# A list scheduler given a more detailed timing model, and a table of priority offsets emptied

## The chip, the cores and the metric

The kernel runs on one core of a Trainium2 chip, as one launch. The metric is the time of one execution on the device in microseconds; the median of several executions counts. Times within the program come from one execution recorded by the hardware profiler. TensorE is called PE, VectorE DVE, ScalarE ACT, GpSimd POOL and SyncE SP, as in the profile.

## The reference

A recurrent attention feeds a two-layer MLP. There are 4 x 8 = 32 heads, 768 positions and 40 features per head:

```python
for t in range(S):
    y[:, :, t] = np.einsum('bhd,bhde->bhe', rt, state)
    Sa = np.einsum('bhde,bhe->bhd', state, at)
    state_decay = state * wt[:, :, None, :] - np.einsum('bhd,bhe->bhde', Sa, bt)
    state = state_decay + np.einsum('bhd,bhe->bhde', vt, kt)
...
x = np.ascontiguousarray(attn_out.transpose(0, 2, 1, 3)).reshape(B * S, H * D)
h = x @ w_in
sp = np.where(h > 20.0, h, np.log1p(np.exp(np.minimum(h, 20.0))))
g = h * np.tanh(sp)
return (g @ w_out).astype(np.float32)
```

`x` is 3072 x 320, `w_in` 320 x 2048, `w_out` 2048 x 320.

## The kernel before

The 768 positions are cut into 12 chunks of 64. Within a chunk the recurrence becomes matrix products and the inverse of a triangular matrix; only the state goes from chunk to chunk. The heads are split into two halves, `be`, and the sixteen pairs of heads of a step into two groups, `g`.

Four kinds of work make up the attention:

- **A fetch**, `pre_a(c, be)`, lines 126 to 203: two loads each of `wa` and `bk` on SP; two scans on DVE (L147, L157) that give the running products of the decays; products of those with a, b and k (L152, L170); eight matmuls of 128 x 128 by 128 x 168 (L186), whose result is taken apart by ACT and DVE (L188 to L193) into `GP` and `HA`; and eight transposes (L202). It writes the running products `P` to memory (L172, POOL's queue). Four fetches serve two chunks.
- **An inversion**, `pre_inv(n)` and `post_inv(n, ...)`, lines 205 to 260, for two chunks at once. First DVE alone: a transpose (L209), thirty rounds of a product and a sum, each needing the one before (L214, L216), and two more transposes (L218, L220). Then PE and ACT put the inverted blocks together (L232, L241, L249 to L251) and multiply them into `KT` (L258, L260).
- **A step**, `step(c)`, lines 265 to 370: the recurrence itself. Its parts run for both groups in the order of `SORD`: `a` brings the state and the values to PE (L277, L284, L286), `b` makes the masked products (L314, L316), `u` and `d` transpose (L293, L304), `c` makes the output and the new state (L334, L339, L342, L343, L346). At its end the loads of the next step are issued on POOL's queue, and the output of the chunk goes to memory (L370).
- **The conversion of the MLP's weights**, `split` and `load_f32`, lines 445 to 516: a piece is loaded to `cv_d` by SP, turned into float32 by one ACT and three DVE instructions (L459 to L463), and split into a high and a low part (L494, L495). `M.early()` does the first of four quarters of `w_in` (3 pieces), `M.first()` the other three (9 pieces), `M.second()` 3 pieces of `w_out`, `M.third()` the last 5. The buffers of `M.first()` lie where those of the fetches were, so it waits for the last fetch; its pieces share one `cv_d`.

The MLP, `Mlp.run`, goes over 12 blocks of 256 rows. `load_x` reads the attention's output back and splits it. For each quarter `q` of the hidden layer, 32 matmuls of 128 x 128 by 128 x 256 (L583) are followed by Mish on ACT (L585), a split (L588, L589), and, three quarters later, 24 matmuls by 320 columns (L603 to L605).

The program is written in one order: fetches 0 to 3, inversion 0, fetches for the next pair, `M.early()`, and then for each pair n of steps, by `ORDER = '0aiA1'`: step 2n, the four fetches of pair n + 2, inversion n + 1, (in the fifth pair) `M.first()`, step 2n + 1. `M.second()` stands ahead of the sixth pair, the MLP at the end.

That is not the order on the engines. At the end of `TileContext` a list scheduler runs the program against a timing model and picks, whenever an engine can take an instruction, the ready one with the best priority. It thereby fixes every engine's queue; on the chip each queue runs in that order, held by semaphores. The priority is the place in the program, and `at(tc, k)` (line 44) changes it for a block: a positive entry of the table `OFF` moves the block forward by about that many places, a negative one back. The keys name the blocks: `I` and `I0` to `I5` the start of an inversion, `J5` and `T1` its second part, `p4` and `P00` to `P11` the fetches, `s0` to `s10` steps, `b0`, `c0`, `u0`, `u1`, `d0`, `d1` parts of every step, `E`, `W` and `V` the three conversions. The model is the framework's default one, which prices each engine's instructions more simply than the other model that it offers.

Most tiles have two buffers, `XL` and `TT` of the inversion one; PSUM has two each for fetches, inversions and the two kinds of step product. Those limits hold whatever the priorities.

Of the kernel before, what the change touches and what calls it, by code (L numbers as in the profile page):

```python
# [34 lines left out]
LA = 2  # L35
ORDER = '0aiA1'

OFF = {'I': 80, 'T1': 80, 'P00': -40, 'P10': 80, 'P11': 40, 'b0': 15, 'c0': 600, 'u0': -15, 'u1': 250, 'd0': 250,
       'd1': 150, 'W': 600, 'V': 400, 'E': 150, 'I0': 600, 'I1': -15, 'I2': 15, 'I3': 150, 'I4': 80, 'p4': 15,
       'I5': -150, 'J5': 600, 's0': 150, 's2': -15, 's3': 80, 's4': 250, 's6': -15, 's7': -40, 's8': 150, 's10': -150}  # L40
SORD = 'a0 b0 u0 d0 a1 b1 u1 d1 c0 c1'


def at(tc, k):
    return tc.high_priority(offset=OFF[k]) if OFF.get(k) else nullcontext()


def layouts(inp, S=768):
    nch = S // C

    def v(x):
        return x[:, :, :S].reshape(4, 2, 2, 2, nch, C, 40)

    r, k, vv, w, a, b = (v(inp[n]) for n in 'rkvwab')
    o = {}
    wt = w.transpose(4, 2, 1, 6, 3, 0, 5).reshape(nch, 2, 2, 40, 8, C)
    wa = np.zeros(wt.shape[:4] + (1040,), np.float32)
    wa[..., :520].reshape(wt.shape[:4] + (8, 65))[..., 1:] = wt
    wa[..., 528:] = a.transpose(4, 2, 1, 6, 3, 0, 5).reshape(nch, 2, 2, 40, 512)
    o['wa'] = wa  # L60
    bt, kt = (x.transpose(4, 2, 1, 6, 3, 0, 5).reshape(nch, 2, 2, 40, 8, 1, C) for x in (b, k))
    bk = np.concatenate([bt, kt], -2)
    bk[:, 1] = np.concatenate([kt, bt], -2)[:, 1]
    o['bk'] = bk.reshape(nch, 2, 2, 40, 8, 128)
    o['rD'] = np.ascontiguousarray(r.transpose(4, 1, 6, 2, 3, 0, 5)).reshape(nch, 2, 40, 16, C)
    o['vD'] = np.ascontiguousarray(vv.transpose(4, 1, 6, 3, 0, 2, 5)).reshape(nch, 2, 40, 8, 128)
    o['vN'] = np.ascontiguousarray(vv.transpose(4, 2, 5, 3, 0, 1, 6)).reshape(nch, 2, C, 16, 40)
    p = np.arange(128)
    cst = np.zeros((128, 328), np.float32)
    cst[:, :128] = np.eye(128)  # L70
    cst[:, 128:192] = (p[:, None] % 64) < np.arange(64)
    cst[:, 192:256] = np.arange(64) < (p[:, None] // 64) * 32 + p[:, None] % 32
    cst[:, 256:296] = (p[:, None] % 64) == np.arange(40)
    cst[:, 296:328] = np.arange(32) < p[:, None] % 32
    o['cst'] = cst
    return o
# [356 lines left out]
def mlp_layouts(inp):  # L433
    wi, wo = inp['moe_w_in'], inp['moe_w_out']
    wi = wi.reshape(2, 2, 2, 40, 2048).transpose(1, 3, 0, 2, 4).reshape(320, 2048)
    a = np.empty((128, 3, 2048), wi.dtype)
    a[:, 0], a[:, 1] = wi[0:128], wi[128:256]
    a[0:64, 2] = a[64:128, 2] = wi[256:320]
    o = {'wi': a.reshape(128, 3, 4, 512).transpose(0, 2, 1, 3), 'wo': wo.reshape(16, 128, 320).transpose(1, 0, 2)}
    o = {n: np.ascontiguousarray(x).reshape(128, -1) for n, x in o.items()}  # L440

    return {n: x.view(np.int64) if x.dtype == np.float64 else x for n, x in o.items()}
# [185 lines left out]
def build(tc, I, out, nch):  # L628
    with ExitStack() as ctx:
        dp = ctx.enter_context(tc.tile_pool(name="dp", bufs=1, space=bass.MemoryType.DRAM))  # L630
        yD = dp.tile([nch, 2, 40, 2, 512], F32, name="yD")
        pD = dp.tile([nch, 2, 40, 2, 520], F32, name="pD")
        M = Mlp(ctx, tc, I, yD, pD, out)
        with ExitStack() as actx:
            attention(actx, tc, I, yD, pD, nch, M)
        M.run(nch)


def launch(**inputs):
    import concourse.bacc as bacc  # L640
    import concourse.tile as tile
    from concourse.bass_utils import run_bass_kernel_spmd

    nch = inputs['r'].shape[2] // C
    arrays = layouts(inputs, nch * C)
    arrays.update(mlp_layouts(inputs))
    nc = bacc.Bacc("TRN2", target_bir_lowering=False, num_devices=1)
    I = {n: nc.dram_tensor("in_" + n, x.shape, mybir.dt.from_np(x.dtype), kind="ExternalInput").ap() for n, x in arrays.items()}
    out = nc.dram_tensor("out_0", (nch * 256, 320), F32, kind="ExternalOutput").ap()
    with tile.TileContext(nc) as tc:  # L650
        build(tc, I, out, nch)
    res = run_bass_kernel_spmd(nc, [{"in_" + n: x for n, x in arrays.items()}], core_ids=[0]).results[0]["out_0"]
    return np.ascontiguousarray(res.reshape(nch, 4, C, 320).transpose(1, 0, 2, 3)).reshape(nch * 256, 320)
# [4 lines left out]
```

## Time and profile before

| What | Value |
|---|---|
| median of 3 runs | 839.51 us (836.24 to 843.57) |
| profiled execution: its span | 843.5 us; the highest of the 3 runs is 843.57 |
| instructions | 18796 |
| PE matmul busy | 748.6 us (89%) |
| PE weight load busy | 695.6 us (82%) |
| DVE busy | 462.0 us (55%) |
| ACT busy | 429.0 us (51%) |
| POOL busy | 103.3 us (12%) |
| DMA | 61.91 MB, mean 73 GB/s |

Shares over the whole span mix stages with different limits, so they are read by stage. In a row of a group of instructions, the columns are: line, engine, operation, output <- inputs, shape and count, then busy time in us with the mean of one in ns, then the idle time of the engine just before them and what ended it. In a row of the timeline: start, length, engine, line, operation, and how many were merged. In a row of stretches: the stretch, its length, the busy time of each engine (with its count of instructions), the granted clock of PE as a share of full speed, the share of the DMA engines, GB/s.

### The profile page before, as it was taken

The page shows a single profiled execution, that of the slowest core. Times are in us where ns is not written, and L with a number is a line of the kernel's source. Part 1 is how long each engine was busy: PE and PEld are TensorE (multiplying, and loading weights), DVE is VectorE, ACT ScalarE, POOL GpSimd, SP SyncE. Part 2 cuts the span into 40 slices and gives each one's busy share as a digit, 9 for nine tenths or more (in the row PEclk, how much of TensorE's full clock was granted, in tenths as well). Part 3 has the DMA queues.
Part 4 walks back from the last instruction along what each step waited for, and adds up shares of the span by engine and source line. Part 5 has one row for each costly group of instructions (what it writes and reads, how often), then busy time and mean ns, then how long its engine had stood idle before and what let it go on. Part 6 is the DMA issues. An engine that isn't in the chain of part 4 may idle for free.

```text
span 843.5 us, 18796 instructions
## 1 busy us (share of the span) xinstructions
PE 748.6 (89%) x7816; PEld 695.6 (82%) x7816; DVE 462.0 (55%) x975; ACT 429.0 (51%) x937; POOL 103.3 (12%) x182
## 2 busy tenths in 40 slices
PE   2645898998989889889799899999999999999998
PEld 2534697887868778778768799999999999999998
DVE  6789879739899658788924639221222222122110
ACT  4533647774586866566738546333333333333331
POOL 8100012113122023221101200000000000000000
PEclk9855689899999999899959999999999999999999
DMA  6422223323423233323425734211120111100000
GB/s 177 134 71 64 74 63 73 90 67 105 129 81 80 66 88 103 82 67 96 123 66 142 179 109 128 54 35 36 38 54 25 31 54 35 35 21 16 16 1 32
DMA packets 58212, 61.91 MB, mean 73 GB/s; under 512 B 25536, under 2 KB 48704, under 8 KB 58128
## 3 DMA queue, kind: packets, MB, share of 16 engines
q1 hardware_dynamic: 49296, 40.94, 17.6%
q0 software_dynamic: 8832, 19.79, 9.5%
q8 instruction: 61, 1.00, 0.5%
q14 instruction: 23, 0.19, 0.1%
HBM read 48.79 MB, written 11.86 MB: 72 GB/s over the span
## 4 chain that ended last, share of the span: by engine, by line
PE 62%; DVE 15%; ACT 15%; issue 5%; DMA 2%; ACTq 0%; DVEq 0%; SPq 0%
PE ph L583 21%; PE po L604 7%; PE po L605 7%; PE po L603 7%; PE pa L186 5%; PE pa L258 4%; PE pq L314 3%; PE pq L334 2%; DVE XL L216 2%; DVE tmp L214 2%; ACT ad L155 2%; PE pu L284 1%; DMA cv_d<-in_wo 1%; DVE P L147 1%; ACT bdT L250 1%
## 5 line engine op out<-in xcount | busy, mean ns | idle before, releaser
L583 PE MATMUL ph<-xh,w_ih 128*128 128x256 f32 x576 | 148.3, 283 | 0.5 <-ACT xh L566 0.5
L585 ACT ACTIVATE g<-ph 128x512 f32<-128x512 f32 x96 | 57.3, 598 | 179.3 <-PE ph L583 179.2
L589 DVE TENSOR_TENSOR gl<-g,gh 128x1024 fp32r<-128x1024 f32 x48 | 58.7, 1225 | 160.7 <-ACT gh L588 160.4
L583 PE MATMUL ph<-xh,w_il 128*128 128x256 f32 x576 | 123.6, 283 | 0.0
L186 PE MATMUL pa<-bk,ad 128*128 128x168 f32 x384 | 85.0, 373 | 42.7 <-DVE bk L170 15.0
L604 PE MATMUL po<-w_ol,gh 128*128 128x320 f32 x384 | 118.8, 310 | 0.1
L605 PE MATMUL po<-w_oh,gl 128*128 128x320 f32 x384 | 118.4, 309 | 0.0
L603 PE MATMUL po<-w_oh,gh 128*128 128x320 f32 x384 | 117.7, 309 | 0.0
L186 PEld LDWEIGHTS pa<-bk,ad 128*128 128x128 f32 x384 | 70.8, 233 | 47.8 <-issue 22.8
L583 PEld LDWEIGHTS ph<-xh,w_ih 128*128 128x128 f32 x576 | 109.3, 190 | 0.7 <-ACT xh L566 0.7
L583 PE MATMUL ph<-xl,w_ih 128*128 128x256 f32 x384 | 101.2, 285 | 0.0
L583 PEld LDWEIGHTS ph<-xh,w_il 128*128 128x128 f32 x576 | 96.3, 190 | 0.0
L583 PEld LDWEIGHTS ph<-xl,w_ih 128*128 128x128 f32 x384 | 73.1, 190 | 0.8 <-issue 0.5
L604 PEld LDWEIGHTS po<-w_ol,gh 128*128 128x128 f32 x384 | 72.1, 188 | 0.5 <-DVE w_ol L495 0.5
L605 PEld LDWEIGHTS po<-w_oh,gl 128*128 128x128 f32 x384 | 72.1, 188 | 0.1
L603 PEld LDWEIGHTS po<-w_oh,gh 128*128 128x128 f32 x384 | 71.8, 188 | 0.0
L258 PE MATMUL pa<-bdT,HA 128*104 128x128 f32 x384 | 57.0, 304 | 9.0 <-ACT bdT L251 7.3
L258 PEld LDWEIGHTS pa<-bdT,HA 128*104 128x104 f32 x384 | 49.9, 190 | 14.4 <-ACT bdT L251 9.1
L216 DVE TENSOR_TENSOR XL<-XL,tmp 128x30 f32<-128x30 f32 (+9 forms) x180 | 59.0, 328 | 2.4
L214 DVE TENSOR_TENSOR tmp<-XL 128x30 f32<-128x30 f32 (+9 forms) x180 | 58.5, 325 | 2.5
L314 PE MATMUL pq<-bdr,UVT 128*128 128x128 f32 x384 | 57.3, 294 | 2.3 <-DVE UVQ L316 1.5
L314 PEld LDWEIGHTS pq<-bdr,UVT 128*128 128x128 f32 x384 | 50.8, 205 | 4.0 <-DVE UVQ L316 1.9
(89 smaller groups left out, 1243.5 us busy)
## 6 DMA issues: line engine op xcount, KB each, us to landing
wa<-in_wa SPq DMA_DIRECT2D x48, 162.5 KB
bk<-in_bk SPq DMA_DIRECT2D x48, 160.0 KB
cv_d<-in_wi SPq DMA_DIRECT2D x12, 512.0 KB
cv_d<-in_wo SPq DMA_DIRECT2D x8, 640.0 KB
pD<-P POOLq DMA_DIRECT2D x48, 81.2 KB, 2.2
VS<-in_vN POOLq DMA_DIRECT2D x24, 160.0 KB, 3.6
UVT<-in_vD POOLq DMA_DIRECT2D x24, 160.0 KB, 3.9
bdr<-in_rD POOLq DMA_DIRECT2D x24, 160.0 KB, 4.4
```

The costliest lines, as they stand in the source:

```text
L155: A.copy(ad[q, :, :, al], a[q].rearrange("p (s k t) -> p s k t", k=2, t=32))
L186: PE.matmul(pt[:, j], ad[:, s0 + j].rearrange("p k a t -> p (k a t)"), bk[:, s0 + j], start=(j == 0), stop=True, skip_group_check=True)
L214: V.tensor_tensor(out=tv, in0=X[:, i + 1:32, i:i + 1].broadcast_to([128, 31 - i, i]), in1=X[:, i:i + 1, 0:i].broadcast_to([128, 31 - i, i] ...
L216: V.tensor_tensor(out=X[:, i + 1:32, 0:i], in0=X[:, i + 1:32, 0:i], in1=tv, op=ALU.add)
L258: PE.matmul(pk[:, j], ha[:, s0 + j], bd[:, s0 + j].rearrange("p a t -> p (a t)"), start=(j == 0), stop=True, skip_group_check=True)
L314: PE.matmul(pq[:, s], UVT[:, g * 4 + s, be * 128:be * 128 + 128], br[:, be, g * 4 + s].rearrange("p a t -> p (a t)"), start=(s == 0), stop ...
L583: PE.matmul(o, w, x, start=(j == 0 and n == 0), stop=(n == 7), skip_group_check=True)
L585: A.activation(g[:, f0:f0 + 2], ph, AF.Mish)
L589: V.tensor_tensor(out=gl, in0=g, in1=gh.bitcast(F32), op=ALU.subtract)
L603: PE.matmul(po[k], gh[:, j, t], oh, start=(f == 0), stop=False, skip_group_check=True)
L604: PE.matmul(po[k], gh[:, j, t], ol, start=False, stop=False, skip_group_check=True)
L605: PE.matmul(po[k], gl[:, j, t], oh, start=False, stop=(f == 15), skip_group_check=True)
```

## The change

The scheduler is told to run the program against the framework's more detailed timing model, and the table of offsets is emptied, so that every block has the priority of its place in the program. The function `at` stays and now does nothing. No instruction is added or removed; tiles, buffers, the order of the program and the assignment to engines and queues stay.

```diff
-OFF = {'I': 80, 'T1': 80, 'P00': -40, 'P10': 80, 'P11': 40, 'b0': 15, 'c0': 600, 'u0': -15, 'u1': 250, 'd0': 250,
-       'd1': 150, 'W': 600, 'V': 400, 'E': 150, 'I0': 600, 'I1': -15, 'I2': 15, 'I3': 150, 'I4': 80, 'p4': 15,
-       'I5': -150, 'J5': 600, 's0': 150, 's2': -15, 's3': 80, 's4': 250, 's6': -15, 's7': -40, 's8': 150, 's10': -150}
+OFF = {}
...
-    with tile.TileContext(nc) as tc:
+    with tile.TileContext(nc, schedule_with_timeline_sim=True) as tc:
         build(tc, I, out, nch)
```

## The prediction

> **What bounds the kernel now.** I read the times of the engines by stage first, then the waits inside the stage that has slack, then the timeline where a chain looked stretched. The stages, with busy time by engine and the granted clock of TensorE:
>
> ```profile
> core 0: us, PE busy (x) PEld busy (x) DVE busy (x) ACT busy (x) POOL busy (x), PEclk, DMA share, GB/s
> 0.00:42.00 42.00, 18.65 (x88) 15.82 (x88) 28.99 (x54) 22.14 (x54) 19.55 (x36) 0.91 0.56 156
> 42.00:105.00 63.00, 36.81 (x266) 30.98 (x267) 56.97 (x139) 27.21 (x79) 5.07 (x10) 0.61 0.23 69
> 105.00:421.00 316.00, 279.15 (x4005) 247.78 (x4004) 251.88 (x632) 212.06 (x541) 67.87 (x120) 0.96 0.34 88
> 421.00:484.00 63.00, 58.23 (x680) 46.61 (x682) 28.60 (x51) 36.70 (x75) 9.86 (x14) 0.84 0.50 125
> 484.00:843.50 359.50, 355.75 (x2786) 354.45 (x2780) 95.59 (x102) 130.93 (x191) 1.00 (x2) 1.00 0.15 43
> ```
>
> The last row is the MLP with the end of the attention: PE is busy for 355.75 of 359.50 us at a clock of 1.00. No order of the queues can shorten it; it only shifts. All that the change can move lies before 484 us. There VectorE sets the start (56.97 of 63 us), and between 105 and 421 us two engines share the limit: PE 279 of 316 us (88%), VectorE 252 (80%). Neither is full, so this stage is limited by the order of its work, and that is what is replaced. What VectorE waits for there and to 484 us:
>
> ```profile
> engine line waited for: us in total, times, longest us
> DVE stn L342 <- PE pq L339: 23.2, 9, 7.7
> DVE UVQ L316 <- PE pq L314: 21.0, 12, 4.6
> DVE HA L191 <- ACT HA L190: 13.9, 17, 2.5
> ```
>
> The two longest, 44.2 us together, are waits for the recurrent steps' own products, not for the work fetched ahead. The steps are thus what the stage can least afford to delay.
>
> **The change part by part.** Nothing is added to or removed from any engine; I take every instruction's duration as it stands, so the sum has only waits. The sum is made against the profiled execution, 843.5 us; the highest of the three runs shown is 843.57 and the median 839.51, so 4.0 us are taken off at the end.
>
> First, the start. The first inversion (30 rounds of L214 and L216) hangs on the first four fetches and stands before the next four in the program too, so it had first call on VectorE with its offset and still has it without. Here is how it ran (timeline of VectorE, first and last lines):
>
> ```profile
> 49.87 2.09 DVE L209 STREAM_TRANSPOSE XL<-GP 128x1024 f32<-128x1024 f32 x1
> 51.84 1.20 DVE L147 TENSOR_TENSOR_SCAN P<-wa,d 128x520 f32<-128x520 f32 x1
> 52.99 0.17 DVE L214 TENSOR_TENSOR tmp<-XL 128x30 f32<-128x30 f32 x1
> 53.02 0.09 DVE L210 MEMSET XL<- 128x32 f32 x1
> 53.08 0.17 DVE L150 COPY w<-P 128x8 f32<-128x8 f32 x1
> 53.15 0.69 DVE L152 TENSOR_TENSOR wa<-wa,P 128x512 f32<-128x512 f32 x1
> 53.75 0.20 DVE L216 TENSOR_TENSOR XL<-XL,tmp 128x30 f32<-128x30 f32 x1
> ...
> 97.25 1.93 DVE L218 STREAM_TRANSPOSE TT<-XL 128x1024 f32<-128x1024 f32 x1
> ```
>
> ```profile
> L216 DVE TENSOR_TENSOR XL<-XL,tmp 128x30 f32<-128x30 f32 (+9 forms) x180 | 59.0, 328 | 2.4
> L214 DVE TENSOR_TENSOR tmp<-XL 128x30 f32<-128x30 f32 (+9 forms) x180 | 58.5, 325 | 2.5
> ```
>
> Its own work is 2.09 + 0.09 + 30 x (0.328 + 0.325) = 21.8 us, but it took 97.25 - 49.87 = 47.4 us, because other ready work was queued after nearly each link. So 25.6 us of fetch work sits inside the chain. Offsets did not prevent that; only the model's view of when a link is ready could. Bounds: 0 if the new model sees it alike, -25.6 if it keeps the chain whole and all of that reaches the end. I take 0, because the inserted work has to be done on the same engine anyway and VectorE is the bound of that stage.
>
> Second, the offsets of the steps and of their parts (`s0`, `s4`, `c0` with 600 and the rest; s2, s6, s7 and s10, being negative, only put steps back). Without them a step with an odd number stands behind four fetches (some 200 instructions, counted in the code) and an inversion (some 260). Its chain has 10 VectorE instructions: 4 of L316, 4 of L342, 2 of L346. Each may now find one longer instruction ahead of it:
>
> ```profile
> L147 DVE TENSOR_TENSOR_SCAN P<-wa,d 128x520 f32<-128x520 f32 x24 | 29.6, 1233 | 0.3
> L170 DVE TENSOR_TENSOR bk<-bk,wa 128x1024 f32<-128x1024 f32 x24 | 29.1, 1214 | 0.1
> ```
>
> That is 10 x 1.23 = 12.3 us for a step at most and 61.5 us for the five (1, 3, 5, 7 and 9), if each lies on the path; 0 if each meets nothing new. What hides it is the PE work fetched ahead, which keeps PE at 88%. Since two thirds of what VectorE idles between 105 and 421 us (316.0 - 251.9 = 64.1) has the size of the step waits above, I count a third as exposed: +20.
>
> Third, `W`, `V` and `E`, which drew the conversion of the MLP's weights forward. SyncE and the chain of the end show it (start, length, what):
>
> ```profile
> 376.11 72.58 SPq L453 DMA_DIRECT2D cv_d<-in_wi  x9
> 455.05 0.33 SPq L453 DMA_DIRECT2D cv_d<-in_wo  x1
> ```
>
> ```profile
> 462.89 3.83 DMA cv_d<-in_wo
> 471.60 4.50 DMA cv_d<-in_wo
> 481.69 0.74 ACT w_oh L494
> ```
>
> Twelve pieces pass through one buffer from 376.1 to 482.4 us, 8.9 us each. Without the offset the first nine stand behind the last inversion on VectorE: at worst they start its own 21.8 us later; at best, once it is done, they run at their own pace. That pace comes from the transfer above and these rows (376 to 484 us):
>
> ```profile
> L463 DVE SCALAR_TENSOR_TENSOR cv_w<-cv_d,cv_w 128x512 int32<-128x512 int32 (+1 forms) x12 | 8.7, 721 | 0.1
> L462 DVE SCALAR_TENSOR_TENSOR cv_w<-cv_m,cv_w 128x512 int32<-128x512 int32 (+1 forms) x12 | 8.6, 719 | 0.2
> L459 ACT ACTIVATE cv_m<-cv_d 128x512 f32<-128x512 f32 (+1 forms) x12 | 8.5, 704 | 2.3 <-DMA cv_d<-in_wi 2.1
> L461 DVE TENSOR_SCALAR cv_w<-cv_m 128x512 int32<-128x512 int32 (+1 forms) x12 | 5.3, 441 | 10.5 <-ACT cv_m L459 10.4
> ```
>
> 3.83 + 0.70 + 0.44 + 0.72 + 0.72 = 6.4 us, so 12 x 2.5 = 30 us could be won back. Bounds -30 to +22; I take +5, near the middle, because the first quarter of the weights (`E`) is ready long before and lets the MLP begin.
>
> Fourth, the one place where the order of PE is plainly bad: from 422 to 431 us two streams alternate two by two.
>
> ```profile
> 424.15 0.31 PE L241 MATMUL pa<-X,GP 32*32 32x32 f32 x2
> 424.39 0.61 PE L334 MATMUL pq<-UVQ,bkn 128*64 128x104 f32 x2
> 424.93 0.31 PE L241 MATMUL pa<-X,GP 32*32 32x32 f32 x2
> ...
> 126.71 0.93 PE L334 MATMUL pq<-UVQ,bkn 128*64 128x104 f32 x16
> ```
>
> ```profile
> 421.00:442.00 21.00, 20.51 (x134) 13.13 (x135) 5.23 (x10) 6.42 (x15) 1.56 (x2) 0.56 0.24 66
> ```
>
> Four matmuls take 0.78 us there, while 16 of L334 in one run take 0.93. In 21 us PE handles 134 matmuls, at a clock of 0.56. The 134 at the 4005 in 279.15 us of the stage before would take 9.3 us, so 11 us are lost. Bounds: -11 if the pattern goes, +11 if there is a second one. I take -5.
>
> This pattern is where the Trainium skill speaks for the new model: its page "TensorEngine Tiling (Array Packing)", section Key Properties, says that a change of tiling mode, not just of tile, drains the array. The trace agrees (0.78 us against about a fifth of that for the same four in longer runs). By that rule the term would be -11 in place of -5, and the sum 854 in place of 860, if the new model knows of the drain.
>
> Sum: 0 + 20 + 5 - 5 = +20, so 863.5 against this execution and, 4.0 less, **860 us** at the median.
>
> **The rivals.** A: the detailed model keeps dependent chains whole, and the result is faster. For it: the 25.6 us of foreign work in the first inversion and the 11 us of alternation are both faults of the old order, and the alternating links were queued in that way in spite of 600 places of offset. Against: the work inside the chain does not vanish. With half of 25.6 gained, the 11 in full, and the steps not delayed: 843.5 - 12.8 - 11 - 4.0 = 816 us. It decides if the first inversion takes under some 35 us and step 0 starts before 105 us.
>
> B: the order changes and the time does not, because buffers (two of most tiles) set it more than priorities do; the terms cancel. For it: PE and VectorE do the same work, 88% and 80% busy, before as after. With a sum of 0 that is 843.5 - 4.0 = 839.5 us. That the flag leaves most of the order as it is ends here too.
>
> C: the inversions themselves fall back behind the fetches, since `I`, `I3` and `I4` pulled them up and in program order the four fetches precede them. Four fetches cost VectorE, each, 2 scans of 1.23, L170 1.21, and by these rows the rest:
>
> ```profile
> L152 DVE TENSOR_TENSOR wa<-wa,P 128x512 f32<-128x512 f32 x24 | 16.4, 685 | 0.0
> L191 DVE TENSOR_TENSOR HA<-pa,cst 128x192 f32<-128x192 f32 (+1 forms) x72 | 23.7, 330 | 25.7 <-ACT HA L190 23.5 <-PE pa L186 2.0
> L145 DVE TENSOR_REDUCE w<-wa 128x8 f32<-128x256 f32 x24 | 9.9, 410 | 0.5 <-PE pa L166 0.4
> L193 DVE TENSOR_TENSOR GP<-GP,cst 128x256 f32<-128x256 f32 x24 | 10.0, 419 | 2.5 <-ACT GP L189 2.5
> ```
>
> 2.46 + 1.21 + 0.69 + 0.99 + 0.41 + 0.42, and 0.5 for small ones, is 6.7 us, 27 us for four. If in two of the four pairs the steps run out of inverted blocks for that long, the time is 843.5 + 54 - 4.0 = 893 us. Against it: an inversion is begun a whole pair of steps ahead, and a pair has some 63 us (316 us for five). C would cost more by the clock: in the stage of 42 to 105 us, where PE is busy for 36.8 of 63, the granted clock is 0.61. By the Trainium skill's "TensorE: Matmul & The Clock Gate", section What's actually happening, the clock is throttled by default and released by recent activity; that agrees with this row, while the row of 421 us (0.56 with PE shown busy for 20.5 of 21) shows that a busy PE by the profile is not enough. As an estimate by that page's 3.4 us of warming up, two such gaps would add about 3.4 us, and C would be 896.
>
> **How the numbers follow.** Forecast (steps delayed, 850 to 880) 0.38; A 0.30; B 0.17; C 0.15. The range leaves out the best end of A (all of 25.6 gained: 803) and the worst of the forecast (61.5 + 22 + 11: 934), about 0.1 each: 812 to 905. The likeliest one's own range is 848 to 885. A difference under 1% can't be told from none here, as the three runs shown spread by 0.9%. Faster by over 1% (under 831): A, 0.30. Within: B, 0.17. Slower (over 848): forecast and C, 0.53.
>
> **What would show it.** In the profile after: the last stage still some 353 to 360 us with PE at 98% or more, wherever it starts; the MLP's first steady row near 500 to 505 us in place of 484; more wait of L316 and L342 for PE, and PE under 88% between 105 us and that point; the first inversion still near 47 us long. The first piece of `cv_d` at 370 to 395 us and the twelfth before 505. Wrong at once would be: a first inversion near 25 us with step 0 well before 105 us (A), or gaps of over 10 us on PE before an L232 (C).

## The result, and the profile after

The changed kernel takes 897.83 us (median of 4 runs, 895.71 to 907.89) against 840.97 us before (836.24 to 843.57, now 4 runs): a ratio of 1.0719, interval [1.0663, 1.0775]. It is slower by 57 us, where 20 had been forecast. Its profiled execution, with a span of 906.1 us, is the slowest of the four.

The stages of the changed kernel, in the view of stretches; the first three rows together, 105 to 543 us, hold what 105 to 484 us held before, and the MLP's steady stage begins at 543 in place of 484:

```profile
core 0: us, PE busy (x) PEld busy (x) DVE busy (x) ACT busy (x) POOL busy (x), PEclk, DMA share, GB/s
105.00:421.00 316.00, 244.52 (x3260) 223.34 (x3261) 214.65 (x527) 173.14 (x449) 56.35 (x100) 0.84 0.26 67
421.00:484.00 63.00, 48.98 (x721) 44.51 (x720) 47.71 (x129) 37.86 (x88) 9.99 (x16) 0.82 0.32 88
484.00:543.00 59.00, 51.80 (x802) 47.50 (x800) 31.41 (x54) 38.23 (x80) 10.41 (x15) 0.93 0.58 135
543.00:906.00 363.00, 358.87 (x2801) 357.48 (x2801) 96.77 (x105) 134.42 (x197) 1.67 (x4) 0.99 0.16 43
```

The last stage is 363.0 us long, 3.5 more than before, and PE fills 98.9% of it. So 59 of the 62.6 us between the two profiled executions were lost before it. In the 316 us from 105 on, PE does 244.5 us of work where it did 279.2, VectorE 214.7 where it did 251.9, ScalarE 173.1 where it did 212.1: everything has slowed down together, and no engine has become the bound. DMA is not full either (0.26). That fits a queue in which something waits at the head. What VectorE waits for, from 40 us to 545 us (total, times, longest):

```profile
DVE w L143 <- DMA wa<-in_wa: 32.8, 14, 4.0
DVE stn L340 <- PE pq L337: 22.6, 12, 6.1
DVE HA L189 <- ACT HA L188: 20.8, 17, 3.0
DVE UVQ L314 <- PE pq L312: 18.5, 13, 5.7
DVE bk L168 <- DMA bk<-in_bk: 16.8, 9, 4.1
```

(Lines after the table of offsets carry a number lower by two than before: L143 is the old L145, the first use of a loaded `wa`; L168 the old L170, which uses the loaded `bk`.) The recurrent steps' waits, L340 and L314, are 41.1 us together, against 47.5 before in the same window (the prediction's 44.2 are for 105 to 484 us). New are the waits for the loads from memory: 32.8 + 16.8 = 49.6 us. Before, no such wait had a row in this window. The chain of work that ended last points the same way; DMA has 12% of it, where it had 2% before. By its tiles, 4% is `bk` and 2% `wa`; the rest is other loads, `bdr` and `cv_d` among them:

```profile
PE 58%; DMA 12%; ACT 7%; DVE 6%; issue 4%; SPq 1%; POOL 0%; DVEq 0%; ACTq 0%; POOLq 0%
```

How such a wait comes about is seen in the timeline of VectorE and SyncE, changed kernel (start, length, engine, line; in brackets the idle time before it and what ended it):

```profile
219.91 1.22 DVE L168 TENSOR_TENSOR bk<-bk,wa 128x1024 f32<-128x1024 f32 x1 [2.06 <-PE pu L291]
...
221.19 0.68 SPq L129 DMA_DIRECT2D wa<-in_wa  x2
...
223.27 0.26 DVE L214 TENSOR_TENSOR XL<-XL,tmp 128x108 f32<-128x108 f32 x1
227.51 0.42 DVE L143 TENSOR_REDUCE w<-wa 128x8 f32<-128x256 f32 x1 [3.98 <-DMA wa<-in_wa]
227.90 0.30 DVE L212 TENSOR_TENSOR tmp<-XL 128x130 f32<-128x130 f32 x1
...
229.42 1.23 DVE L155 TENSOR_TENSOR_SCAN wa<-wa,d 128x519 f32<-128x519 f32 x1
```

L168 is the last to read a buffer of `wa`. When it ends (221.13), SyncE at once issues the load of the next fetch but one into that buffer. VectorE's queue holds a few short pieces after it, runs dry at 223.53, and stands for 3.98 us before the first use of that load, 6.3 us after its issue. Ready work stands behind: the next link of an inversion (L212), whose input was done at 223.53, and the second scan (L155) and the L168 (at 235.64) of the fetch in between come only after it. Over the 20 fetches from 40 us on, the work on VectorE between the end of such an L168 and the first use of the refilled buffer has a median of 3.6 us in the changed kernel and 6.9 before (summed from the two timelines). In the 14 waits for `wa` in the list above, 3.6 to 7.8 us pass from the issue of the load to that first use, with a median of 4.6.

The theory from this was: **the detailed model's queue order puts the first use of a load too early behind the release of its buffer, and every queue behind that wait loses the time.** One rival was that the loss comes from the offsets. The other, that the inversion is stretched: the first one now lasts from 54.69 to 118.85, 64.2 us where it was 47.4, and PE has no matmul at all from 100 to 120 us. In the expectations below, M blames the model's own order, O the offsets, S the stretched inversions. From the second group on, D blames the waits for loads, P takes them for a symptom of an order that is bad for other reasons, and D+ says that they are a part of the loss and that the rest of the order loses 10 to 20 us besides.

One number below needs a word: of the four executions of the kernel with the first rule and three buffers for `wa`, three took 877.09 to 880.05 us and one, the profiled one, 1408.83, so its waits are not read.

### The profile page after: what moved, and what is told of

The parts are those of the page before. It is cut to its first block, busy times and chain, and to the rows that moved or that the text cites. A ratio compares the mean times of both kernels' runs of the same rounds, so it can differ in the third digit from the quotient of the medians.

```text
span 906.1 us, 18831 instructions
## 1 busy us (share of the span) xinstructions
PE 759.5 (84%) x7816; PEld 719.4 (79%) x7816; DVE 466.1 (51%) x975; ACT 429.9 (47%) x937; POOL 104.1 (11%) x182
## 4 chain that ended last, share of the span: by engine, by line
PE 58%; DMA 12%; ACT 7%; DVE 6%; issue 4%; SPq 1%; POOL 0%; DVEq 0%; ACTq 0%; POOLq 0%
PE ph L581 18%; PE po L601 6%; PE po L602 6%; PE po L603 6%; PE pq L312 5%; PE pa L256 4%; DMA bk<-in_bk 4%; PE pq L332 3%; DMA wa<-in_wa 2%; DMA bdr<-in_rD 2%; PE pa L184 2%; PE pa L239 2%; DMA cv_d<-in_wi 2%; ACT bdT L247 2%; ACT bdT L248 2%
## 5 line engine op out<-in xcount | busy, mean ns | idle before, releaser
L184 PE MATMUL pa<-bk,ad 128*128 128x168 f32 x384 | 87.9, 386 | 39.1 <-DVE HA L189 20.3
L184 PEld LDWEIGHTS pa<-bk,ad 128*128 128x128 f32 x384 | 74.7, 244 | 44.1 <-DVE HA L189 22.6
L312 PE MATMUL pq<-bdr,UVT 128*128 128x128 f32 x384 | 62.0, 328 | 9.4 <-DMA bdr<-in_rD 5.1
L312 PEld LDWEIGHTS pq<-bdr,UVT 128*128 128x128 f32 x384 | 58.0, 238 | 11.3 <-ACT UVT L284 4.8
L332 PE MATMUL pq<-UVQ,bkn 128*64 128x104 f32 (+1 forms) x768 | 51.2, 276 | 16.4 <-ACT yev L341 15.5
L212 DVE TENSOR_TENSOR tmp<-XL 128x30 f32<-128x30 f32 (+9 forms) x180 | 58.4, 324 | 3.3
L332 PEld LDWEIGHTS pq<-UVQ,bkn 128*64 128x64 f32 x768 | 42.0, 152 | 22.6 <-ACT yev L341 17.5
## 6 DMA issues: line engine op xcount, KB each, us to landing
wa<-in_wa SPq DMA_DIRECT2D x48, 162.5 KB
```

The costliest lines, as they stand in the source:

```text
L184: PE.matmul(pt[:, j], ad[:, s0 + j].rearrange("p k a t -> p (k a t)"), bk[:, s0 + j], start=(j == 0), stop=True, skip_group_check=True)
L212: V.tensor_tensor(out=tv, in0=X[:, i + 1:32, i:i + 1].broadcast_to([128, 31 - i, i]), in1=X[:, i:i + 1, 0:i].broadcast_to([128, 31 - i, i] ...
L312: PE.matmul(pq[:, s], UVT[:, g * 4 + s, be * 128:be * 128 + 128], br[:, be, g * 4 + s].rearrange("p a t -> p (a t)"), start=(s == 0), stop ...
L332: PE.matmul(py[be * 64:be * 64 + 64, 2 * j + al, 0:n], BKN[c, be][:, u * 40:u * 40 + 64], UVQ[be][:, u, 0:n], start=(j == 0 and al == 0), ...
```

## The experiments

All kernels were timed against the kernel before on the same chip, which ran at 838.36, 840.03, 839.73 and 838.58 us in the four groups. "Load waits" is VectorE's time waiting for `wa` and `bk` between 40 and 545 us.

**The two halves of the change, each alone.** The first has the detailed model and the old table:

```diff
-OFF = {}
+OFF = {'I': 80, 'T1': 80, 'P00': -40, 'P10': 80, ...
```

> The detailed model with all offsets kept. Theory O (the loss comes from the missing offsets, which let fetches into the inversions): near the kernel before, 835 to 850 us. Theory M (the loss comes from the model's own order, which puts instructions that wait for late loads ahead of the inversion's links): near the kernel after, 885 to 905 us. Its queue of VectorE has 6 fetches begun inside the first inversion, as the kernel after has, so M expects that inversion to last 60 us or more; O expects it to matter little.

The second has the old model and the empty table:

```diff
-    with tile.TileContext(nc, schedule_with_timeline_sim=True) as tc:
+    with tile.TileContext(nc) as tc:
```

> The default model with the table of offsets emptied. Theory O: 885 to 905 us, as slow as the kernel after. Theory M: 840 to 860 us. Its queue of VectorE has 6 fetches begun inside the first inversion too (4 in the kernel before); if it is the count of fetches inside that matters, the first inversion lasts over 55 us here as well.

Measured: the model alone 893.99 us, ratio 1.0654 [1.0598, 1.0709], load waits 49.7 us. The offsets alone 839.95 us, 1.0021 [0.9989, 1.0053]. So the offsets are worth nothing that can be measured under the default model and at most some 4 us under the detailed one (897.83 against 893.99, with intervals that overlap), and the model is the loss. The first falls where M expected it, the second 0.05 us below. The default model's order without offsets, in the groups of instructions between 40 and 545 us (count, then busy and mean ns, then idle time before them):

```profile
L168 DVE TENSOR_TENSOR bk<-bk,wa 128x1024 f32<-128x1024 f32 x21 | 25.5, 1215 | 0.8 <-DMA bk<-in_bk 0.8
L143 DVE TENSOR_REDUCE w<-wa 128x8 f32<-128x256 f32 x20 | 8.1, 406 | 0.8 <-PE pa L164 0.8
```

And the changed kernel's:

```profile
L143 DVE TENSOR_REDUCE w<-wa 128x8 f32<-128x256 f32 x20 | 8.3, 417 | 35.6 <-DMA wa<-in_wa 32.8 <-PE pa L164 2.8
L168 DVE TENSOR_TENSOR bk<-bk,wa 128x1024 f32<-128x1024 f32 x21 | 25.6, 1221 | 20.6 <-DMA bk<-in_bk 16.8 <-PE pu L291 3.9
```

The same instructions with the same durations, the same loads, the same empty table: only the place in the queue differs. One reuse of a buffer in the default order, timeline of the second kernel:

```profile
61.09 1.22 DVE L168 TENSOR_TENSOR bk<-bk,wa 128x1024 f32<-128x1024 f32 x1
...
62.37 0.68 SPq L129 DMA_DIRECT2D wa<-in_wa  x2
...
70.07 1.22 DVE L168 TENSOR_TENSOR bk<-bk,wa 128x1024 f32<-128x1024 f32 x1
...
71.51 0.41 DVE L143 TENSOR_REDUCE w<-wa 128x8 f32<-128x256 f32 x1
```

Here 9.1 us lie between issue and use, VectorE is busy nearly all through, and the L168 of the fetch in between comes first. Over its 20 fetches the work in this place has a median of 7.6 us, more than 13 of the 14 loads above took.

**Inversions kept whole.** If the stretched inversion were the cause, forbidding other work in it should win. In the first kernel the second four fetches stand behind the first inversion on VectorE; in the second, each inversion also precedes the fetches of its pair, and all of those wait for it:

```diff
-        V.transpose(T1, TT[0:64])
+        M.last = V.transpose(T1, TT[0:64])
...
-            pre_a(2 + u // 2, u % 2)
+            with tc.issue_after(M.last.ins):
+                pre_a(2 + u // 2, u % 2)
```

> The kernel after, with the VectorE instructions of the second four fetches queued behind the first inversion, so that nothing stands inside it. Theory S (the stretched first inversion delays everything behind it, 64 us in place of some 24): step 0 starts 30 to 40 us earlier and the time falls by 20 to 35 us, to 863 to 878 us. Rival: the fetches are only done later and the steps run out of them, so the time stays at 890 to 900 us.

```diff
-ORDER = '0aiA1'
+ORDER = '0iaA1'
...
-                    with at(tc, 'p%d' % n), at(tc, 'P%d%d' % (c, be) if n else ''):
+                    with tc.issue_after(M.last.ins) if n else nullcontext():
```

> The kernel after, with each inversion written ahead of the fetches of the pair after it and these queued behind it on VectorE, so that all six inversions hold few or no foreign instructions. Theory S: all inversions last 22 to 32 us but the last, and the steps never wait for one for long: 835 to 860 us. Rival: fetches come too late, PE runs out of work, and the time is over 885 us.

Measured: 914.09 us, 1.0893 [1.0838, 1.0948], and 926.65 us, 1.1052 [1.0977, 1.1126]: both slower than the change itself, the first even beyond its rival's 890 to 900. The timeline of the first of them:

```profile
53.16 2.10 DVE L207 STREAM_TRANSPOSE XL<-GP 128x1024 f32<-128x1024 f32 x1
...
77.29 1.90 DVE L216 STREAM_TRANSPOSE TT<-XL 128x1024 f32<-128x1024 f32 x1
```

The inversion takes 24 us instead of 64, and step 0 ends about 26 us earlier. But the fetches taken out of it have to run afterwards, the second inversion ends at 201 us instead of 159, and PE waits longer for inverted blocks. PE's wait for the inversion, from 40 to 545 us, in the changed kernel, with the first inversion whole and with all of them whole:

```profile
PE pa L230 <- DVE TT L216: 29.7, 3, 22.8
```

```profile
PE pa L230 <- DVE TT L216: 63.0, 6, 25.3
```

```profile
PE pa L230 <- DVE TT L216: 96.8, 6, 26.3
```

These two kernels also have load waits, 57.0 and 32.9 us, so their own times do not settle what a stretched chain costs. The second kernel of the group before does: with the default model and no offsets the first inversion lasts 52.7 us, with the starts of six fetches inside it as in the changed kernel, and the time is 839.95 us. VectorE's work inside the chain is the same in both (48.9 and 49.4 us); the changed kernel's chain is 11.5 us longer, and 12.0 us of waits for `wa` lie inside it:

```profile
50.49 2.09 DVE L207 STREAM_TRANSPOSE XL<-GP 128x1024 f32<-128x1024 f32 x1
...
103.19 1.88 DVE L216 STREAM_TRANSPOSE TT<-XL 128x1024 f32<-128x1024 f32 x1
```

```profile
DVE w L143 <- DMA wa<-in_wa: 12.0, 6, 3.8
```

The foreign work inside the chain was thus not the fault, and the theory of the stretched inversion fell; the stretch beyond 52.7 us is itself made of load waits.

**More buffers.** A third buffer for `wa` releases each one fetch earlier:

```diff
-    wab = [cp.tile([128, 1040], F32, name=f"wa{i}") for i in range(NWA)]
+    wab = [cp.tile([128, 1040], F32, name=f"wa{i}") for i in range(3)]
...
-        wa, bk, ad = wab[n % NWA], bkb[n % NWA], adb[n % 2]
+        wa, bk, ad = wab[n % 3], bkb[n % NWA], adb[n % 2]
```

> The kernel after with three buffers for wa in place of two, so that its loads can start one fetch earlier. Theory D (VectorE's waits for late loads, 32.8 us for wa and 16.8 us for bk between 40 and 545 us, are the loss; the default order has next to none): the waits for wa fall under 10 us and the time by 20 to 35 us, to 863 to 878 us. Rival P (the waits only show where an order that is bad for other reasons has its slack): the waits fall, the time stays at 885 to 905 us.

> The same third buffer for wa under the default model without offsets, as a control. Theory D: VectorE does not wait for loads there anyway, so 835 to 845 us. Rival P: the same. Below 830 us both would be wrong about the loads in the default order.

Measured: with the detailed model 874.06 us, 1.0435 [1.0374, 1.0497]; with the default one 836.97 us, 0.9966 [0.9932, 1.0]. Some 24 us came back under the detailed model, within what the theory of the loads expected. The waits for `wa` fell from 32.8 to 6.3 us, those for `bk` rose to 24.5. Three buffers of both (with one buffer fewer, seven, for `BKN`, to make room):

```diff
-NBKN = 8
+NBKN = 7
-NWA = 2
+NWA = 3
```

> The kernel after with three buffers for wa and for bk (and seven in place of eight for the transposed copy bkn, for room). Theory D: nearly all waits of VectorE for loads go, and the time falls by 40 to 55 us, to 843 to 858 us. Rival P: 885 to 905 us.

> The same under the default model without offsets, as a control for the buffers. Both theories: 832 to 846 us.

Measured: 873.27 us, 1.0423 [1.0373, 1.0473], and for the control 855.15 us, 1.0187 [1.0147, 1.0226]. Both lie outside what either theory expected: the edit itself costs 15 us under the default model, and under the detailed one 18.0 us of load waits (all for `wa`) were left; why was not settled in either case. Against its control the detailed model lost 18 us.

**The order put right by a rule.** If the place in the queue is what counts, no buffer is needed: it is enough to forbid what the timeline of the changed kernel shows. In the next kernel the VectorE work of a fetch stands behind the L168 of the fetch before it:

```diff
     def pre_a(c, be):
+        with tc.issue_after(M.prev.ins) if M.prev else nullcontext():
+            fetch(c, be)
...
-        V.tensor_tensor(out=bk4, in0=bk4, ...
+        M.prev = V.tensor_tensor(out=bk4, in0=bk4, ...
```

> The kernel after with one rule on the order of VectorE's queue: a fetch's instructions stand behind the product with bk of the fetch before it. Nothing is computed, loaded or buffered otherwise. In the order after, VectorE has only 3.6 us of work (median) between the release of a buffer of wa and the first use of what is loaded into it; in the default order without offsets 7.7. Theory D (the load takes longer than the model's order leaves for it): the waits for loads, 49.6 us, fall under 20, and the time by 25 to 45 us, to 853 to 873. Rival P (the model's order is bad for other reasons): the time stays over 885 us.

> The same rule under the default model without offsets, where VectorE hardly waits for loads. Both theories: 834 to 850 us; the rule costs a little at most.

Measured: 875.85 us, 1.0405 [1.0333, 1.0476], and 839.31 us, 0.9995 [0.9959, 1.0031]. The rule costs the default order nothing and gives the detailed one 22 us, 3 us short of what D expected. The scheduler plans the whole program anew around the rule, so other places in the queues can differ too; the controls under the default model are there for that. The waits for `wa` are gone, those for `bk` are now 30.6 us, not under 20. The groups of instructions with the detailed model:

```profile
L174 DVE TENSOR_TENSOR bk<-bk,wa 128x1024 f32<-128x1024 f32 x21 | 25.7, 1222 | 35.2 <-DMA bk<-in_bk 30.6 <-PE pu L297 2.9 <-PE pq L318 1.7
L149 DVE TENSOR_REDUCE w<-wa 128x8 f32<-128x256 f32 x20 | 8.2, 412 | 0.0
```

The wait went to the next load whose first use stood early. Two more kernels of that group: the rule with three `wa`, and a rule that puts a fetch behind the last VectorE work on the fetch before (the mask of `GP`).

> The detailed model, the rule of the run before the last, and a third buffer for wa. Theory D: the waits for wa go, those for bk fall under 15 us, and the time is 840 to 860 us. Rival P: over 870 us, as with the third buffer alone (874).

> The detailed model with a wider rule: a fetch's instructions stand behind the last VectorE instruction of the fetch before it, the mask of GP, which itself waits for PE and ACT. Theory D: waits for loads under 5 us; the time 845 to 870 us, since the fetches no longer overlap each other. Rival P: over 885 us.

Measured: 877.18 us (the median of the three near one another), 1.0426 [1.0349, 1.0502], a miss for D and within what P expected. That freeing `wa` is of no use while `bk` has the waits would explain it, but no trace at this time shows it. And 869.21 us, 1.0314 [1.024, 1.0388], as D expected, with no load waits left but 46.2 us of waits on L195 for ScalarE (26.7 in the default order without offsets); each fetch is now serial.

The last group took away the waits for `bk` too. Once by the rule with three buffers of both, once by a second rule: a fetch's own `bk` product stands behind the mask of `GP` of the fetch before. Then the controls:

```diff
-        M.prev = V.tensor_tensor(out=bk4, in0=bk4, ...
+        with tc.issue_after(M.mask.ins) if M.mask else nullcontext():
+            M.prev = V.tensor_tensor(out=bk4, in0=bk4, ...
```

> The detailed model with three buffers for wa and bk (and seven for bkn) and the rule that a fetch stands behind the product with bk of the fetch before. Its control is the default order with the same buffers, 855 us. Theory D (the waits for loads are the whole loss): waits under 5 us and 852 to 862 us. Theory D+ (they are part, the model's order loses some 10 to 20 us besides): waits under 5 us and 864 to 875 us.

> The detailed model with two rules on VectorE's queue: a fetch stands behind the product with bk of the fetch before, and its own product with bk behind the mask of GP of the fetch before. Theory D: the waits for bk, 30.6 us under the first rule alone, fall under 10, and the time to within 10 us of its control, the next run: 838 to 855 us. D+: waits under 10, time 858 to 872.

> The same two rules under the default model without offsets, the control: no waits for loads, 836 to 852 us by both theories.

> The default model without offsets under the wide rule of the earlier run (a fetch behind the mask of GP of the fetch before), which under the detailed model has no waits for loads and takes 869 us. Theory D: the rule itself is what costs there, and this run takes 860 to 870 us too. D+: 840 to 852 us, so that 17 to 29 us of the detailed order have another cause.

Measured, in this order: 865.73 us, 1.0317 [1.0229, 1.0405]; 856.05 us, 1.0201 [1.0135, 1.0267]; 844.81 us, 1.0062 [1.0028, 1.0096]; 884.15 us, 1.053 [1.0455, 1.0604]. The first fits D+. The second falls between the two ranges, 1 us above D's and 2 us below that of D+. The last fits neither: the rule that makes each fetch serial costs the default order 44 us, more than either theory allowed. The second of them has the detailed model, two buffers of each and both rules. Its groups have no idle time ahead of either use:

```profile
L175 DVE TENSOR_TENSOR bk<-bk,wa 128x1024 f32<-128x1024 f32 x21 | 25.5, 1217 | 0.0
L149 DVE TENSOR_REDUCE w<-wa 128x8 f32<-128x256 f32 x20 | 8.2, 408 | 0.0
```

And its VectorE works at nearly the pace of the default order again: in the same 316 us it does 248.8 us of work, the default order 249.7, the changed kernel 214.7. The stretch of this kernel, then that of the default order without offsets:

```profile
105.00:421.00 316.00, 265.73 (x3835) 240.32 (x3836) 248.80 (x612) 202.66 (x523) 62.15 (x110) 0.89 0.30 82
```

```profile
105.00:421.00 316.00, 274.53 (x4110) 246.67 (x4112) 249.67 (x622) 213.94 (x544) 65.89 (x116) 0.94 0.31 83
```

Put together, each kernel with the detailed model against the default order under the same edit (differences of the medians above; the first against the offsets taken out alone; the control of the row marked * has the buffers without the rule):

| Edit | load waits, us | detailed minus default, us |
|---|---|---|
| none (the change) | 49.6 | 58 |
| three `wa` | 30.8 | 37 |
| first rule | 30.6 | 37 |
| three of both | 18.0 | 18 |
| both rules | 0 | 11 |
| first rule, three of both * | 0 | 11 |
| each fetch serial | 0 | -15 |

In the rows with load waits the difference is as large as these or up to 8 us larger; in the rows without, it lies between 11 and -15. So the waits carry most of the loss, though not one for one: from the row with three of both to the next of these buffers, 18 us of waits went and 7.5 us of time. With both rules, which cost the default order 5 us, 47 of the 58 us are gone (42 in the time itself, 897.83 to 856.05). The remaining 11 us, which turn to a gain of 15 in the last row, are differences in the rest of the order, and which these are was not settled. Also open is why the detailed model orders the fetches so: that it takes the loads for shorter than they are would explain it, but this was only inferred from the order. No version beat the kernel before by more than the measurement can tell; the best has three `wa` and the default model, 0.9966 [0.9932, 1.0].

## Why the prediction was right or wrong

The direction was right, and 897.83 lies inside 812 to 905, but outside the likeliest case's own 848 to 885. The mechanism behind the sum was wrong, and the right direction was luck: neither term that made the sum positive, +20 and +5, is what the runs showed.

**The step that failed** is its frame: "I take every instruction's duration as it stands, so the sum has only waits", with the waits looked for on the steps, the inversion and the conversion. From the list of waits in the kernel before it concludes that "the steps are thus what the stage can least afford to delay". The loads of `wa` and `bk` have no term, and no reason is given. The profile of before has next to no wait for them (0.5 and 0.1 us of idle time before L145 and L170, in rows that the prediction shows); that only showed that some 7 us of other work lay queued ahead of each first use. A new model can take that cover away, and it did: 3.6 us of work (median) against loads that took 3.6 to 7.8 us. The term that was left out measured about 47 us.

**The start, taken at 0 (bounds -25.6 to 0).** The range excluded a longer chain, and it became longer, 64.2 us. In the timeline of the changed kernel six of the waits for `wa` lie inside it, 12.0 us together; the two longest:

```profile
54.69 2.09 DVE L207 STREAM_TRANSPOSE XL<-GP 128x1024 f32<-128x1024 f32 x1
...
70.60 0.42 DVE L143 TENSOR_REDUCE w<-wa 128x8 f32<-128x256 f32 x1 [3.81 <-DMA wa<-in_wa]
...
102.44 0.42 DVE L143 TENSOR_REDUCE w<-wa 128x8 f32<-128x256 f32 x1 [3.35 <-DMA wa<-in_wa]
...
118.85 1.91 DVE L216 STREAM_TRANSPOSE TT<-XL 128x1024 f32<-128x1024 f32 x1
```

The reason given for not taking the gain, that "the inserted work has to be done on the same engine anyway", fits the runs: the kernel with this chain at 24 us was slower, and the one with 52.7 us and no such waits as fast as before.

**The steps' offsets, +20 (0 to 61.5).** Wrong. The table emptied under the old model costs 0.2%, within its interval of nothing, and the steps' waits did not rise in the changed kernel (41.1 us against 47.5). The lower bound, 0, was the nearest. That a step which meets a scan of 1.2 us loses it to idle time that it has anyway would explain it, and was not shown.

**The weights' conversion, +5.** The forecast was the first piece at 370 to 395 us and the twelfth before 505. SyncE in the changed kernel:

```profile
440.02 59.08 SPq L451 DMA_DIRECT2D cv_d<-in_wi  x9
516.09 0.33 SPq L451 DMA_DIRECT2D cv_d<-in_wo  x1
...
532.28 0.52 SPq L451 DMA_DIRECT2D cv_d<-in_wo  x1
```

It begins 64 us later than before, and the twelfth piece is issued at 532.28: both missed. Its nine first pieces take 59.08 us where they took 72.58, but the twelve are done at 545.4, 105 us after the start, as against 106 before. So it is shifted with the rest, and not quicker. That the offset keeps it early does not hold in the default order: without offsets it starts at 376.5 us too, is done at 465.2, 17 us sooner than with them, and the time of the kernel is the same. Under the detailed model the offsets do start it 30 us earlier (410 us), and the time is 893.99 in place of 897.83.

**PE's alternation, -5 (-11 to +11).** The pattern went, but with the offsets and not by the model. After 100 us, L241 and L334 stand next to each other on PE 28 times in the kernel before and 17 times with the detailed model and the old table; without the table once in the changed kernel and never in the default order, where PE's clock from 421 to 442 us is 1.00. Yet that default order takes 839.95 us, so no gain of 11 us shows in the time; what the rest of the table was worth is in that figure too. By the Trainium skill's rule on mode changes ("TensorEngine Tiling (Array Packing)", section Key Properties) the term would have been -11; the pattern's end without a gain that can be measured does not bear that price out.

**The last stage**, 353 to 360 us at 98% or more: 363.0 us at 98.9% and a clock of 0.99, so right in kind and 3 us off. Its start was forecast at 500 to 505 us and came at 543. PE under 88% after 105 us: right, 77% to 421 us.

**The rivals.** A said that whole chains make it faster; the two kernels that kept them whole were the slowest of all. B's observation that buffers set the order more than priorities do was the nearest to the mechanism, but its conclusion, no change, holds for the offsets only. C's 893 us is near the measured time, and its sign came, a gap of over 10 us on PE before an L232 (L230 now): one of 22.8 us. But it was to be two of 27, from inversions that fall behind the fetches. PE's wait for the inversion has 29.7 us in three pieces between 40 and 545 us, and the long one stands at the end of the first inversion, which load waits had stretched by 12.0 us.

## What to carry to other kernels

A profile without waits for a load says that enough work is queued ahead of its first use, not that the load is free: before anything reorders queues, measure for each recycled buffer the time from its release to its next use on the engine and compare it with the time from issue to use of that load. When a change slows all engines together and fills none, look for a wait at the head of an in-order queue with ready work behind it. A rule on the order can guard against it, but one rule may only move the wait to the next buffer: here the first cost the default order nothing and left 30.6 us, two took all the waits away for 5 us, and the widest did so for 44. And a long dependent chain with other work between its links is not by itself a loss on an engine that needs that work anyway.

## What was not expected of the hardware

The two loads of a `wa` buffer, 162.5 KB each, took 3.6 to 7.8 us from issue to first use in the 14 waits (median 4.6), though the DMA engines were busy for only 26% of the time from 105 to 421 us. By the Trainium skill's "DMA: Bandwidth & Descriptors", section Anatomy of one DMA — SWDGE (gpsimd) path, a transfer on GpSimd's path takes a fixed 2.0 us and the bytes at 436 GB/s; as an estimate by that page, 325 KB would take 2.8 us. These loads are issued by SyncE, so the formula is not for this path; the trace's times are 1.3 to 2.8 times as long, and with 2.8 us a cover of 3.6 us would have been enough at the median.

The idle time went with a lower clock. In the 20 us in which PE had no matmul, the changed kernel's view of stretches shows its clock at half speed. Over the whole of 105 to 545 us it is 0.85; in the kernel before, the stages up to the MLP's steady one, 105 to 484 us, have 0.94. What the lower clock cost in time was not separated:

```profile
100.00:120.00 20.00, 0.00 (x0) 0.00 (x0) 15.31 (x39) 0.00 (x0) 1.02 (x2) 0.50 0.14 45
105.00:545.00 440.00, 346.75 (x4802) 316.69 (x4802) 294.50 (x709) 251.12 (x620) 77.41 (x132) 0.85 0.32 80
```

That the clock falls to half in an idle stretch agrees with the Trainium skill's "TensorE: Matmul & The Clock Gate", section What's actually happening.
